# Hash bits of a group's first head copied within SBUF instead of through DRAM, with a shorter warm-up: attention and routed MLP on one Trainium2 core

## The chip, the cores and the metric

The kernel runs on one core of one Trainium2 chip. The metric is the device time of one execution in microseconds (us). Every run quoted here is fast: none was over 1.5% above the fastest of its kernel, the mark beyond which a run is set aside as slow. Times inside an execution come from a profile of one execution and count from the start of its span. The granted clock is the share of TensorE's full clock that the profile shows as given to it: 1.00 is full, 0.50 half.

## The reference, cut to what matters

Attention is restricted by a hash: a query sees only the keys whose 6 hash bits equal its own. A routed MLP with 8 experts follows.

```python
q_bits = (np.einsum('bhsd,dk->bhsk', q, proj) > 0)      # 6 bits per query; k_bits the same
mask = q_bucket[:, :, :, None] == k_bucket[:, :, None, :]
scores = np.where(mask, scale * (q @ k^T), -1e9)
attn = softmax(scores); attn_out = attn @ v             # 4 batches, 8 heads, 768 positions, 64 columns
...                                                     # then _moe_ref: Sinkhorn routing, 8 experts
```

## The kernel before

The eight heads of a batch are two groups of four heads, so there are eight groups. A group is 24 units (4 heads x 6 key tiles). A unit is one pair of score matmuls (`st`), one exponential on ScalarE (`pt`) and six value matmuls (`num`). The mask has no instructions of its own: each key and each query is extended from 64 rows to 71 by its bits, so that the score matmul itself pushes down the pairs that differ.

The preparation of a group, `prepare(n)`, runs while the group before is computed. It transposes k and q on VectorE, casts them on GpSimd, copies ("stacks") each head's 32-row pieces into place by DMA, and computes the bits: TensorE hashes (`pr`), VectorE compares (`bt`). The bits of all four heads lie in `bt` in the wrong partitions. They go to a scratch tensor in DRAM (`put_bits`) and come back head by head (`get_bits`).

```python
def eng(name, h):                 # who issues the small transfers
    return nc.scalar if n == 0 and name == "q" and h < 3 else nc.sync
def put_bits():
    bt = d["bt"]
    dss["kq"] = scr.tile([2, 2, HG, 8, HT], F16, tag="ds", name="ds")           # DRAM
    pin(nc.sync.dma_start(out=dss["kq"].rearrange("n j h r t -> (n j h r) t"), in_=bt))
def get_bits(name, h):
    pin(eng(name, h).dma_start(out=d[name][D:KR, h, :].rearrange("r (j t) -> r j t", j=2),
                               in_=dss["kq"]["kq".index(name), :, h, 0:NB + 1, :].rearrange("j r t -> r j t")))
...
fetch(0, "kqv", nc.sync)
warm = ops.tile([P, 512], F32, tag="o", name="warm")
for x in range(42):               # matmuls on nothing: 0.43 us each at first, 0.22 us from 8.9 us on
    if x == 18:
        for _ in prepare(0): pass
    pin(nc.tensor.matmul(warm, ident, ..., start=True, stop=True))
...
for u in range(len(units) + 1):   # u-th unit; i = u % 24; prepare(n + 1) advances at chosen i
    ...
    pts[u + 1] = scores(*units[u + 1])
    values(u - 1 ...)
```

Bulk loads (k, q and v of the next group at 768 KB each, expert weights at 1 MB) are issued by GpSimd. On the page of the kernel before, the queue of its transfers took 46.5% of the time of the core's 16 DMA engines, those of SyncE and ScalarE 7.6% and 0.5%.

The softmax here doesn't subtract the row's maximum and nothing guards it: scores larger than these inputs give would overflow.

## Time and profile before

| | before |
|---|---|
| time, median of 3 runs | 786.95 us (786.22 to 787.77) |
| span of the profiled execution | 783.6 us (785.36 timed) |
| first exponential of groups 0, 1, 2, 3 | 21.26, 42.22, 65.12, 91.05 us |
| from group 3's first exponential to the end | 692.6 us |

The profiled execution was a little faster than every timed run of this kernel.

From the page of the kernel before: the span, TensorE's busy time, the granted clock in tenths over 40 slices, and the chain of work that ended last.

```profile
span 783.6 us, 16645 instructions
...
PE 757.7 (97%) x6286; PEld 521.1 (66%) x6286; DVE 530.2 (68%) x1198; ACT 509.2 (65%) x1022; POOL 310.8 (40%) x314
...
PEclk9979999999999999999999999999999999999999
...
PE 84%; ACT 7%; DVE 4%; DMA 2%; issue 1%; SPq 1%; POOL 1%; ACTq 0%; POOLq 0%; DVEq 0%
```

TensorE is the bound over the whole span: 97% busy, and 84% of the chain that ended last. The 7 in the third slice (39 to 59 us) is the only dent in the clock.

From the timeline of TensorE: start, length, what, count. In brackets stand the idle time before it and what ended it.

```profile
15.55 5.35 PE L600 MATMUL warm<-va,ident 128*128 128x512 f16 x24
20.74 0.81 PE L507 MATMUL st<-qs,ks 71*128 71x384 f16 x4
...
41.64 0.48 PE L507 MATMUL st<-qs,ks 71*128 71x384 f16 x2 [2.08 <-DMA ks<-ds]
```

The scores start as the warm-up ends. At the first head of group 1 TensorE stood still for 2.08 us, until bits came back from DRAM (`ds`).

From the timeline of the DMA issues on SyncE (SPq), the write to DRAM and the read back, for group 1 and then group 2:

```profile
33.91 0.53 SPq L412 DMA_DIRECT2D ds<-bt  x1
...
39.61 0.27 SPq L415 DMA_DIRECT2D ks<-ds  x1
...
55.26 0.35 SPq L412 DMA_DIRECT2D ds<-bt  x1
...
61.98 0.27 SPq L415 DMA_DIRECT2D ks<-ds  x1
```

A read is issued as soon as its write has landed (39.61 after 39.60 us, 61.98 after 61.97 us). So the write took 5.7 us for group 1 and 6.7 us for group 2, both beside bulk loads (DMA share 1.00 and 1.07). For group 0, with no bulk load in the way (share 0.44), it took 1.66 us. Group 2's bits landed at 64.0 us and its first scores began at 64.53 us.

From the stretch table, the 3.41 us before the clock fell and the half-clock time in thirds: stretch, its length, busy us (count) of PE, PEld, DVE, ACT, POOL, then the granted clock, DMA share and GB/s.

```profile
39.59:43.00 3.41, 1.35 (x17) 0.88 (x18) 0.00 (x0) 1.47 (x3) 0.00 (x0) 1.00 0.16 40
43.00:46.41 3.41, 3.33 (x29) 2.31 (x29) 3.35 (x5) 2.85 (x5) 2.18 (x3) 0.50 0.27 69
46.41:49.83 3.42, 3.42 (x29) 2.16 (x27) 0.56 (x2) 2.30 (x4) 2.81 (x5) 0.50 0.83 277
49.83:53.24 3.41, 3.41 (x25) 1.06 (x24) 0.75 (x2) 1.26 (x2) 2.25 (x4) 0.50 1.02 218
```

After the stretch with the wait the clock is at half for 10.24 us (43.00 to 53.24 us). Group 1 takes 22.9 us from its first exponential to the next group's; group 0, without its wait, took 18.9.

### The profile page before, as it was taken

How to read it: one execution, taken by the hardware profiler on the slowest of the kernel's cores; microseconds unless marked ns; L12 is line 12 of the kernel's file. 1: busy time of each engine (PE TensorE's matmuls, PEld its weight loads, DVE VectorE, ACT ScalarE, POOL GpSimd, SP SyncE). 2: the span in 40 equal slices, each digit the busy share in tenths (PEclk: the TensorE clock that was granted, in tenths of full speed). 3: DMA queues.
4: the chain of work that ended last, by engine and by line, in shares of the span. 5: the costliest groups of instructions: out<-in, count | busy, mean ns of one | idle time of the engine just before them, and what ended most of it. 6: DMA issues, size and time to landing. Idle time of an engine off the chain costs nothing.

```text
span 783.6 us, 16645 instructions
## 1 busy us (share of the span) xinstructions
PE 757.7 (97%) x6286; PEld 521.1 (66%) x6286; DVE 530.2 (68%) x1198; ACT 509.2 (65%) x1022; POOL 310.8 (40%) x314
## 2 busy tenths in 40 slices
PE   6989999999999999999999999999999999999996
PEld 2556656666654676677777777777777777777763
DVE  3435646654449877777777777777777777777774
ACT  0868767677854777766666666666666666666660
POOL 5745346437500133344434334333444443324220
PEclk9979999999999999999999999999999999999999
DMA  5976557463003364486468647764864496443335
GB/s 148 256 167 180 133 164 186 121 151 87 2 1 55 54 108 82 88 155 109 88 111 153 108 82 132 132 115 81 150 119 93 94 166 109 81 82 82 82 82 134
DMA packets 42088, 88.56 MB, mean 113 GB/s; under 512 B 7384, under 2 KB 22360, under 8 KB 42008
## 3 DMA queue, kind: packets, MB, share of 16 engines
q0 software_dynamic: 27440, 71.06, 46.5%
q1 hardware_dynamic: 13545, 15.33, 7.6%
q10 hardware_dynamic: 1023, 1.11, 0.5%
q8 instruction: 49, 0.80, 0.4%
q14 instruction: 31, 0.25, 0.1%
HBM read 53.14 MB, written 7.08 MB: 77 GB/s over the span
## 4 chain that ended last, share of the span: by engine, by line
PE 84%; ACT 7%; DVE 4%; DMA 2%; issue 1%; SPq 1%; POOL 1%; ACTq 0%; POOLq 0%; DVEq 0%
PE a L725 18%; PE a L249 17%; PE d L725 13%; PE y L249 9%; PE st L507 6%; PE d L249 4%; PE hp L565 4%; ACT pt L510 4%; PE num L523 3%; PE yp L575 3%; PE pr L396 2%; PE hp L322 1%; ACT acc L240 1%; PE yp L306 1%; DVE hT L734 1%
## 5 line engine op out<-in xcount | busy, mean ns | idle before, releaser
L734 DVE CUSTOM_DVE_ANT_0 hT<-d,u 128x384 f16<-128x384 f32 x336 | 185.6, 553 | 96.2 <-ACT u L730 95.5
L253 ACT ACTIVATE vt<-a,p 128x256 f32<-128x256 f32 x324 | 153.6, 474 | 148.7 <-PE a L249 148.5
L510 ACT ACTIVATE pt<-st 128x768 f16<-128x768 f32 x192 | 146.4, 809 | 64.7 <-PE st L507 45.4
L730 ACT COPY u<-a 128x384 f32<-128x384 f32 x336 | 161.2, 480 | 23.5 <-PE a L725 19.9
L288 POOL DMA_DIRECT2D acc<-vt x72 | 61.4, 853 | 267.9 <-ACT vt L253 112.8
L249 PEld LDWEIGHTS <-hT 128*128 128x128 f16 x1296 | 126.3, 97 | 50.7 <-DVE hT L734 1.1
L249 PE MATMUL a<-t,hs 128*128 128x256 f16 x972 | 145.8, 272 | 2.0 <-ACT vt L253 1.5
L249 PEld LDWEIGHTS <-hs 128*128 128x128 f16 x972 | 94.8, 98 | 38.3 <-issue 2.8
L725 PEld LDWEIGHTS <-t 128*128 128x128 f16 x896 | 87.7, 98 | 36.3 <-issue 0.6
L725 PE MATMUL d<-xd,t 128*128 128x384 f16 x448 | 109.4, 326 | 0.3 <-DVE hT L734 0.3
L725 PE MATMUL a<-xT,s 128*128 128x384 f16 x448 | 109.4, 326 | 0.1
L507 PE MATMUL st<-qs,ks 71*128 71x384 f16 x384 | 96.0, 332 | 7.1 <-ACT pt L510 3.5
L249 PE MATMUL y<-t,hT 128*128 128x256 f16 x648 | 97.1, 272 | 0.0
L257 DVE SCALAR_TENSOR_TENSOR acc<-y,p,acc 128x256 f32<-128x256 f32 x162 | 77.5, 478 | 11.4 <-PE y L249 11.4
L523 PEld LDWEIGHTS <-pt 128*128 128x128 f16 x1152 | 61.8, 99 | 27.6 <-issue 2.2
L725 PEld LDWEIGHTS <-s 128*128 128x128 f16 x672 | 65.5, 98 | 17.5 <-issue 2.3
L523 PE MATMUL num<-va,pt 128*128 128x65 f16 x1152 | 67.8, 195 | 0.6 <-ACT pt L510 0.6
L764 ACT ACTIVATE hT<-a 128x384 f16<-128x384 f32 x112 | 54.1, 483 | 1.8 <-PE a L725 1.7
L725 PE MATMUL a<-xd,s 128*128 128x384 f16 x224 | 54.3, 323 | 0.8 <-ACT u L730 0.6
L725 PE MATMUL d<-xT,t 128*128 128x384 f16 x224 | 54.7, 326 | 0.0
L725 PE MATMUL a<-xT,t 128*128 128x384 f16 x224 | 54.7, 326 | 0.0
L507 PEld LDWEIGHTS <-ks 71*128 71x128 f16 x384 | 33.8, 99 | 30.5 <-issue 16.4
(100 smaller groups left out, 954.7 us busy)
## 6 DMA issues: line engine op xcount, KB each, us to landing
acc<-vt POOLq DMA_DIRECT2D x72, 512.0 KB, 4.7
t<-in_moe_w_dram POOLq DMA_DIRECT2D x24, 512.0 KB, 7.2
acc<-in_k_dram POOLq DMA_DIRECT2D x7, 768.0 KB, 5.6
acc<-in_q_dram POOLq DMA_DIRECT2D x7, 768.0 KB, 12.1
v<-in_v_dram POOLq DMA_DIRECT2D x28, 192.0 KB, 5.4
out_dram<-acc SPq DMA_DIRECT2D x82, 64.0 KB
t<-in_moe_w_dram POOLq DMA_DIRECT2D x4, 1024.0 KB, 10.9
ks<-t SPq DMA_DIRECT2D x64, 48.0 KB
```

What stands on the lines that cost most here:

```text
L249: pin(nc.tensor.matmul(dst, hq[hn][:, fo, :], wq[wn][:, fo, :], start=first and fo == 0, stop=fo == FH - 1, skip_group_check=True))
L253: pin(nc.scalar.activation(out=vt[:, k], in_=a, func=Act.Copy, scale=p))
L257: pin(nc.vector.scalar_tensor_tensor(out=dst, in0=src, scalar=p, in1=dst, op0=Alu.mult, op1=Alu.add))
L288: pin(nc.gpsimd.dma_start(out=acc[:, b, i], in_=vt, accum_op=Alu.add))
L507: pin(nc.tensor.matmul(st[:, i, 0:HT], d["k"][0:KR, h, kt * P:(kt + 1) * P], d["q"][0:KR, h, i * HT:(i + 1) * HT], start=True, stop=True))
L510: pin(nc.scalar.activation(out=pt, in_=st[:, :, 0:HT], func=Act.Exp, scale=scale))
L523: pin(nc.tensor.matmul(num[:, j * (D + 1):(j + 1) * (D + 1)], pf[:, j * P:(j + 1) * P], va[:, h, kt, :], start=(kt == 0 and j == 0), stop= ...
L565: pin(nc.tensor.matmul(hp[:, 0:HT], w1[:, do, fo * P:(fo + 1) * P], xT[:, do, b * S + t * HT:b * S + (t + 1) * HT], start=(do == 0), stop= ...
L725: pin(nc.tensor.matmul(bk, wq[wn][:, do, f * P:(f + 1) * P], xq[xn][:, do, :], start=first and do == 0, stop=do == 1, skip_group_check=True))
L730: pin(nc.scalar.copy(t, bk))
L734: pin(add(TENSOR_ADD_SAT, out=dst, in0=bk, in1=u, s0=3e38, s1=0.0))
L764: pin(nc.scalar.activation(out=hT[:, f, hi], in_=a, func=Act.Relu))
```

## The change

The intent is to shorten the way of the bits that are needed first. Head 0 of groups 0, 1 and 2 gets its bits by four small copies straight from `bt`. The DRAM way remains for the other heads. The warm-up loses 8 matmuls before the first hash and 2 after it, and ScalarE issues q's heads 0 and 1 of group 0 only; head 2 goes to SyncE.

```diff
-            return nc.scalar if n == 0 and name == "q" and h < 3 else nc.sync
+            return nc.scalar if n == 0 and name == "q" and h < 2 else nc.sync
 ...  # get_bits now always on nc.sync
+        def move_bits(name):
+            for x in range(2):
+                p = 64 * "kq".index(name) + 32 * x
+                pin(eng(name, 0).dma_start(out=d[name][D:KR, 0, x * HT:(x + 1) * HT], in_=d["bt"][p:p + NB + 1, :]))
 ...
+        if n < 3:
+            move_bits("k")
+            move_bits("q")
         put_bits()
         if n == 0:
             stack("k", 1)
             stack("q", 1)
-            for h in range(2):
-                get_bits("k", h)
-                get_bits("q", h)
+            get_bits("k", 1)
+            get_bits("q", 1)
 ...
-        for h in range(2 if n else 0):
+        for h in range(1 if n < 3 else 0, 2 if n else 0):
             get_bits("k", h)
             get_bits("q", h)
 ...
-    for x in range(42):
-        if x == 18:
+    for x in range(32):
+        if x == 10:
```

More of the change, by code (lines that the diff above doesn't have):

```diff
@@ L414, in get_bits @@
         def get_bits(name, h):
-            pin(eng(name, h).dma_start(out=d[name][D:KR, h, :].rearrange("r (j t) -> r j t", j=2),
+            pin(nc.sync.dma_start(out=d[name][D:KR, h, :].rearrange("r (j t) -> r j t", j=2),
                                        in_=dss["kq"]["kq".index(name), :, h, 0:NB + 1, :].rearrange("j r t -> r j t")))
+        def move_bits(name):
+            for x in range(2):
+                p = 64 * "kq".index(name) + 32 * x
+                pin(eng(name, 0).dma_start(out=d[name][D:KR, 0, x * HT:(x + 1) * HT], in_=d["bt"][p:p + NB + 1, :]))
         def cast_v():
```

## The prediction

> **What bounds the kernel now.** TensorE: the page has PE busy 97% of 783.6 us (786.95 timed), and the chain that ended last is PE for 84%. The change touches only the first 70 us, where three stretches are lost to something else:
> 1. Start. The first score matmul is at 20.74 us (timeline). By the stretch table, warm-up fills PE before it: 18 matmuls to 10.68 us (0.43 us each cold, 0.22 warm), the key hash (1.48 us), 24 more from 15.55 to 20.9 us. By semaphore landings the first head's bits arrive at 19.6 to 20.4 us. VectorE waits 3.5 us for the key hash, though q landed at 9.57 us.
> 2. Head 0 of group 1. PE idles 2.08 us (39.56 to 41.64 us; waits view: "PE st <- DMA ks<-ds"). Its bits left VectorE at 33.86 us; the write to DRAM took 33.91 to 39.60 us behind bulk loads, the read back 1.4 us.
> 3. Then the granted clock falls to 0.50 (42.96 to 53.2 us, stretch table). [...] six 65-column matmuls went from 0.35 to 0.54 us[...]. From first exponential to the next group's, group 1 takes 22.9 us; group 0, warm, 18.9 without its stall: 3.9 us lost.
>
> **What the change does.** It removes 10 warm-up matmuls, 8 of them before the key hash, which is then bound by the transposes (8.62 us) or the tenth warm-up (8.75 us): 1.8 us earlier, with q's transposes and hash behind it. For head 0 of groups 0 to 2, two DRAM hops (1.66 + 1.8 us quiet, 5.7 + 1.4 loaded) become one hop of four small copies (estimate 1.5 us quiet, 5 to 6 loaded; 0.3 to 0.6 us of issue each). The DRAM write follows them, needed only for head 1, 4.4 us later. ScalarE issues 6 transfers instead of 9; SyncE takes q's head 2, which delays q's head 3, whose landing (29.72 us) releases the next group's casts.
>
> **On the critical path.** Start: scores at about 18.7 us, set by the warm-up's end (bits at 16.7): -1.9 us; only -0.5 if the clock stays cold. Group 1: consumers come 2 us earlier, data 1 to 1.7, the skipped hop gives 1.5 to 2: stall about 1 us (-1). Clock: so short a stall probably doesn't halve it (60%): -3.9 if so, -2.3 expected. Group 2: the copies land just in time. All of it carries to the end, as later work is paced by PE. Sum about -5 us.
>
> **Predicted: 782.0 us, range 778.0 to 786.8; faster by over 2% 0.02, within 2% 0.97, slower 0.01.**
>
> **What would show it.** First score matmul at 18 to 19.5 us; PE's wait at group 1 under 1.3 us; granted clock 1.00 from 40 to 55 us; group 1 about 19 us; after 70 us only shifted; ds no longer releasing head 0.
>
> **What would make it wrong.** [...] 22 second-burst matmuls at 0.43 us would then end as late as before. The copies queue behind the same stacked transfers and bulk loads ([...] SyncE copies took 1.9 us quiet, 5 to 7 us beside bulk loads), so the stall may stay at 2 us, and the half clock with it: about 785.

Passages that no trace or run of this case shows are cut, where marked. -1.9 (start), -1 (wait at group 1) and -2.3 us (clock) make -5.2, called about -5. In the case that heads "what would make it wrong" the clock stays cold after the first ten warm-up matmuls. In the profile of the kernel before, the clock stayed at 1.00 after a wait of 1.82 us during the warm-up (12.09 to 13.91 us) and fell after the one of 2.08 us at group 1.

## The result, and the profile after

| | before | after |
|---|---|---|
| time, median of 4 runs each | 786.59 us (786.16 to 787.77) | 781.97 us (780.54 to 782.59) |
| ratio, 95% interval | | 0.9936 (0.9918 to 0.9955) |
| span of the profiled execution | 783.6 us | 780.0 us |
| first exponential of group 0 | 21.26 us | 18.54 us (-2.72) |
| group 0: to group 1's first | 20.95 us | 23.39 us (+2.44) |
| group 1: to group 2's first | 22.90 us | 19.40 us (-3.50) |
| group 2: to group 3's first | 25.93 us | 26.03 us (+0.10) |

Ratios here and below are the mean time of one kernel's fast runs over that of the other's of the same rounds, so they are not quite the ratio of the quoted medians. The time fell by 0.6%, which counts as the same at the 2% mark but lies clear of 1. The last four rows add up to -3.7 us, as the two spans differ; the timed medians differ by 4.6 us, as the profiled execution of the kernel before was faster than its timed runs.

The page after:

```profile
span 780.0 us, 16636 instructions
...
PE 754.0 (97%) x6276; PEld 519.0 (67%) x6276; DVE 531.3 (68%) x1198; ACT 509.1 (65%) x1022; POOL 310.6 (40%) x314
...
PEclk9899999999999999999999999999999999999998
...
PE 83%; ACT 8%; DVE 4%; issue 2%; POOL 1%; DMA 1%; SPq 0%; ACTq 0%; POOLq 0%; DVEq 0%
```

The dent in the clock is still there. It has moved from the third slice to the second. TensorE's timeline after:

```profile
13.26 4.92 PE L607 MATMUL warm<-va,ident 128*128 128x512 f16 x22
18.02 0.82 PE L514 MATMUL st<-qs,ks 71*128 71x384 f16 x4
...
28.34 0.80 PE L514 MATMUL st<-qs,ks 71*128 71x384 f16 x2 [1.79 <-DMA qs<-ds]
```

The start came 2.7 us earlier and the wait at group 1 is gone. In its place stands a new wait of 1.79 us, at the first scores of head 2 of group 0, for q's bits. That is the head which the change handed from ScalarE to SyncE. SyncE's issues around it:

```profile
18.36 1.17 SPq L390 DMA_DIRECT2D qs<-t  x2
19.58 1.55 SPq L390 DMA_DIRECT2D ks<-t  x2
21.17 0.53 SPq L415 DMA_DIRECT2D ks<-ds  x1
21.75 0.32 SPq L415 DMA_DIRECT2D qs<-ds  x1
```

Head 2's q bits were issued at 21.75 us and landed at 28.21 us, with group 1's bulk loads under way since 18.52 us. Before, ScalarE issued them at 20.29 us, ahead of the bulk loads (20.82 us), and they landed at 22.16 us.

The stretch table after, the 3.41 us before the clock fell and the two halves of the half-clock time:

```profile
24.80:28.21 3.41, 1.65 (x23) 1.07 (x21) 2.83 (x5) 2.47 (x4) 0.64 (x1) 1.00 1.06 231
28.21:31.62 3.41, 3.28 (x21) 1.31 (x22) 0.56 (x1) 0.81 (x1) 2.64 (x5) 0.50 0.74 150
31.62:35.03 3.41, 3.41 (x26) 1.30 (x24) 1.93 (x4) 1.24 (x2) 3.41 (x6) 0.50 1.32 276
```

The pair of wait and half clock that stood at 40 to 53 us stands at 26 to 35 us now. The last lines are SyncE's for group 2, followed by its first scores, which waited for nothing:

```profile
52.73 1.53 SPq L421 DMA_DIRECT2D ks<-bt  x2
54.36 1.43 SPq L421 DMA_DIRECT2D qs<-bt  x2
55.84 0.44 SPq L412 DMA_DIRECT2D ds<-bt  x1
56.42 1.20 SPq L390 DMA_DIRECT2D ks<-t  x2
62.10 0.28 SPq L415 DMA_DIRECT2D ks<-ds  x1
```
```profile
60.74 0.48 PE L514 MATMUL st<-qs,ks 71*128 71x384 f16 x2
```

The four copies landed at 58.09 to 59.77 us. The DRAM write behind them landed at 62.09 us, so by that write head 0 would have had its bits at about 64 us (an estimate; head 1's landed at 64.3 to 64.5 us), more than 3 us after the scores began. The run moves_g01 below has no copies ahead of the write: 63.55 us.

### The profile page after: what moved, and what is told of

The parts are those of the page before. It is cut to its first block, busy times and chain, and to the rows that moved or that the text cites. A ratio compares the mean times of both kernels' runs of the same rounds, so it can differ in the third digit from the quotient of the medians.

```text
span 780.0 us, 16636 instructions
## 1 busy us (share of the span) xinstructions
PE 754.0 (97%) x6276; PEld 519.0 (67%) x6276; DVE 531.3 (68%) x1198; ACT 509.1 (65%) x1022; POOL 310.6 (40%) x314
## 4 chain that ended last, share of the span: by engine, by line
PE 83%; ACT 8%; DVE 4%; issue 2%; POOL 1%; DMA 1%; SPq 0%; ACTq 0%; POOLq 0%; DVEq 0%
PE a L732 18%; PE a L249 17%; PE d L732 13%; PE y L249 9%; PE st L514 6%; ACT pt L517 5%; PE d L249 4%; PE hp L572 4%; PE num L530 3%; PE yp L582 3%; PE pr L396 2%; PE hp L322 1%; ACT acc L240 1%; PE yp L306 1%; DVE hT L741 1%
## 5 line engine op out<-in xcount | busy, mean ns | idle before, releaser
L517 ACT ACTIVATE pt<-st 128x768 f16<-128x768 f32 x192 | 146.2, 809 | 61.2 <-PE st L514 44.3
L737 ACT COPY u<-a 128x384 f32<-128x384 f32 x336 | 161.2, 480 | 22.9 <-PE a L732 20.3
## 6 DMA issues: line engine op xcount, KB each, us to landing
acc<-in_q_dram POOLq DMA_DIRECT2D x7, 768.0 KB, 11.8
```

The lines of the kernel that those rows point to most:

```text
L517: pin(nc.scalar.activation(out=pt, in_=st[:, :, 0:HT], func=Act.Exp, scale=scale))
L737: pin(nc.scalar.copy(t, bk))
```

## The experiments

The total came out as predicted, but by another way: a late wait gone, an early one come. The question is which part of the change bought the 0.6%. The theories at the outset: (S) the start and the skipped hop at group 1 are two gains that add up; (I) the new wait at head 2 comes from the hand-over to SyncE and costs what it shows; (C) the half clock is a cost of its own. Their rivals say that each group waits for its own data, whatever its predecessor gains.

Twelve kernels were run in three batches, each with 5 rounds beside the kernel before, on three further chips. On these the kernel before was slower and more scattered (medians 788.5 to 788.7 us, 785 to 793 us) than on the first. All results are correct. The granted clock of the kernel before was 0.982 to 0.995 there, mostly lower in the slower runs, against 0.991 in the one profile of the kernel before, from the first chip. So its executions differ in how much half clock they hold, and what that profile shows, the half microsecond of slack at group 2 too, is one execution; none was profiled on these chips. The columns g0 to g3 are the first exponentials of the groups in the profiled execution, in us; the last column is where the clock was at half after it had first come up, in the first 100 us.

| run | ratio (95%) | g0 | g1 | g2 | g3 | half clock, us |
|---|---|---|---|---|---|---|
| before | 1 | 21.26 | 42.22 | 65.12 | 91.05 | 43.0-53.2 |
| after | 0.9936 (0.9918-0.9955) | 18.54 | 41.93 | 61.33 | 87.36 | 28.2-35.0 |
| after_again | 0.9940 (0.9908-0.9973) | 21.40 | 44.97 | 64.37 | 90.66 | 13.7-17.2, 30.8-37.6 |
| warm_only | 0.9989 (0.9956-1.0022) | 18.65 | 40.41 | 62.78 | 92.23 | 38.7-45.5, 62.6-72.8 |
| moves_only | 0.9940 (0.9912-0.9968) | 22.31 | 42.59 | 62.84 | 91.91 | 43.7-47.1, 91.5-94.9 |
| moves_g01 | 0.9995 (0.9966-1.0023) | 18.88 | 41.19 | 64.69 | 92.51 | 28.9-32.3, 63.0-69.9 |
| moves_g12 | 0.9935 (0.9915-0.9955) | 18.46 | 42.66 | 61.70 | 87.65 | 28.1-34.9 |
| moves_g2 | 0.9932 (0.9913-0.9950) | 19.00 | 43.85 | 63.02 | 88.98 | 29.1-36.0 |
| before_hot | 1.0001 (0.9969-1.0032) | 21.68 | 43.08 | 66.83 | 97.14 | 64.3-78.0 |
| keepwarm | 0.9930 (0.9904-0.9956) | 19.71 | 43.00 | 64.52 | 90.44 | 44.3-51.1 |
| gets_first | 0.9980 (0.9951-1.0008) | 18.32 | 43.48 | 67.00 | 92.93 | 27.8-31.2, 41.4-55.1 |
| act3 | 0.9926 (0.9903-0.9950) | 19.41 | 43.22 | 62.27 | 89.11 | 20.8-34.5 |
| act3_hot | 0.9918 (0.9893-0.9943) | 20.43 | 40.17 | 59.86 | 86.70 | none |
| act3_hot_m4 | 0.9926 (0.9903-0.9948) | 20.36 | 41.43 | 63.40 | 89.34 | 39.9-50.1 |

The profiled executions of moves_only, before_hot, keepwarm and act3 were the slowest of their six (787.88, 791.38, 784.71 and 783.58 us), those of moves_g01 and moves_g12 the fastest (786.51 and 781.95 us).

### warm_only: the shorter warm-up alone

```diff
 # on the kernel before
-    for x in range(42):
-        if x == 18:
+    for x in range(32):
+        if x == 10:
```

> The kernel before with the shorter warm-up alone (32 matmuls, the first hash after 10); bits still go by DRAM, ScalarE still issues 9 transfers. Theory S (the start and the group-1 hop are two separate gains): first exponential about 2.5 us earlier (18.5 to 19 us instead of 21.26), because the warm-up's end, not the bits, set the start; the idle of about 2 us at the first head of group 1 and the half clock after it (group 1 about 22.9 us long) stay; total about -2.5 us. Rival M (the start came from the moved bits): first exponential at 20 us or later, total 0 to -1 us. Head 2 of group 0 has no idle, since ScalarE still issues its q.

Measured: 787.33 us median, ratio 0.9989. The start came 2.6 us earlier, as Theory S had it, and head 2 didn't wait. But the gain is not to be told from zero. TensorE's waits for DMA in this profile:

```profile
39.52 0.80 PE L507 MATMUL st<-qs,ks 71*128 71x384 f16 x2 [2.58 <-DMA ks<-ds]
62.20 0.48 PE L507 MATMUL st<-qs,ks 71*128 71x384 f16 x2 [1.51 <-DMA ks<-t]
```

Group 2 still began 2.3 us earlier than before (62.78 against 65.12 us). It waited 1.51 us at its first head, the clock halved there, and group 2 took 29.45 us instead of 25.93. What the start had given was lost in group 2, a place that the prediction had not priced.

### moves_only: the moves alone

```diff
 # on the changed kernel: ScalarE's share (h < 3, and get_bits by eng) and the warm-up (42, 18) as before
-            return nc.scalar if n == 0 and name == "q" and h < 2 else nc.sync
+            return nc.scalar if n == 0 and name == "q" and h < 3 else nc.sync
-            pin(nc.sync.dma_start(out=d[name][D:KR, h, :]...
+            pin(eng(name, h).dma_start(out=d[name][D:KR, h, :]...
-    for x in range(32):
-        if x == 10:
+    for x in range(42):
+        if x == 18:
```

> The changed kernel with the old warm-up (42, hash after 18) and ScalarE issuing q's heads 0 to 2 as before: only the moves within SBUF are new. Theory S: start unchanged (first exponential about 21.2 us), no idle at head 2 of group 0 (its q bits issued by ScalarE, landing by about 22 us), no idle of more than 0.5 us at the first head of group 1, no half clock between 20 and 60 us; group 0 and group 1 about 19 us each; total about -5.5 us. Rival M: first exponential at 19.5 us or earlier.

Measured: 783.96 us median, ratio 0.994, the same as the whole change. The start was not earlier (22.31 us), so Rival M is out. But groups 0 and 1 were not free of waits, as Theory S had it: TensorE waited at the first head of group 1 and the clock halved once between 20 and 60 us.

```profile
41.67 0.48 PE L514 MATMUL st<-qs,ks 71*128 71x384 f16 x2 [1.07 <-DMA qs<-bt]
```
```profile
40.27:43.68 3.41, 1.90 (x26) 1.24 (x25) 0.59 (x2) 2.14 (x4) 0.33 (x1) 1.00 0.25 72
```

Later in the same profile, that of the slowest of the six runs, group 3, whose head 0 still went by DRAM, waited 2.09 us at its first scores (91.22 us), and the clock halved there too: the same loss one group further on.

So the moves carry the gain and the start needn't contribute. Which of the three moves is told by the next runs.

### moves_g01, moves_g12 and moves_g2: which group's move counts

```diff
 # on the changed kernel; the range of get_bits changed to match
-        if n < 3:
+        if n < 2:            # moves_g01;   n in (1, 2) for moves_g12;   n in (2,) for moves_g2
             move_bits("k")
             move_bits("q")
```

> The changed kernel with the moves left out for group 2 alone (its head 0 goes by DRAM again). Theory W (the move for group 2 is what lets the earlier groups' gain reach the end): TensorE waits 1 us or more for group 2's first bits, as in the run with the shorter warm-up alone (1.5 us), the clock may halve after it, and group 2 starts or runs 1.5 to 5 us later than in the changed kernel; total -0.5 to -3 us against before. Rival N (group 2's move does nothing): no wait there, total as the changed kernel within 1 us.

> The changed kernel with the moves left out for group 0 alone (its head 0 goes by DRAM again; shorter warm-up and SyncE's share kept). Theory W (group 0's move is idle, since the warm-up's end sets the start and groups 1 and 2 wait for their own data): first exponential within 0.5 us of the changed kernel's for the same clock phase, no wait over 0.5 us at the first heads of groups 1 and 2, total 0.992 to 0.996 of before. Rival Z (all three moves count): first exponential over 1 us later after the warm-up's end and total within 2 us of before.

> The changed kernel with the moves left out for groups 0 and 1, kept for group 2 alone. Theory X (the move for group 1 counts as well): TensorE waits 1 us or more for DMA at the first head of group 1, and the clock may halve after it, so that group 1's first or last exponential is 1 to 4 us later than with both moves; total -0.5 to -3 us against before. Rival Y (group 2's move alone carries the gain, since group 1 in the changed kernel is slowed by group 0's wait at head 2 anyway): no wait over 0.5 us at the first head of group 1, total as the changed kernel, 0.992 to 0.996.

Measured: without group 2's move, 0.9995: the whole gain is gone (787.80 us median). Without group 0's, 0.9935; with group 2's alone, 0.9932 (783.12 and 783.17 us, same chip). So, beside the shorter warm-up and SyncE's share, which all three runs have, the move for group 2 carries the gain, and the moves for groups 0 and 1 add nothing that these runs can see. In moves_g01 TensorE's waits were

```profile
28.78 0.70 PE L514 MATMUL st<-qs,ks 71*128 71x384 f16 x2 [1.89 <-DMA qs<-ds]
...
63.80 0.80 PE L514 MATMUL st<-qs,ks 71*128 71x384 f16 x2 [3.83 <-DMA ks<-ds]
```

and in moves_g2

```profile
29.46 0.80 PE L515 MATMUL st<-qs,ks 71*128 71x384 f16 x2 [2.45 <-DMA qs<-t]
43.27 0.48 PE L515 MATMUL st<-qs,ks 71*128 71x384 f16 x2 [0.84 <-DMA ks<-ds]
```

The wait of 0.84 us at group 1 lies between what Theory X (1 us or more) and Rival Y (under 0.5 us) had expected; the total sides with Y. The 3.83 us of moves_g01 is the DRAM way of group 2, met by a group 1 that finished on time. This table of landings, read from the profile's semaphore events, shows it (issue to landing, us; for reads and copies the earliest issue and the latest landing of head 0):

```
            write to DRAM     read back         copies in SBUF    first scores of group 2
before      55.26 to 61.97    61.98 to 64.00    -                 64.53, no wait
moves_g01   51.75 to 58.62    58.68 to 63.55    -                 63.80, after 3.83 us of waiting
before_hot  53.77 to 60.83    60.84 to 65.60    -                 65.94, after 4.42 us of waiting
after       (62.09)           -                 52.73 to 59.77    60.74, no wait
```

Both hops ran beside bulk loads. In before, the write landed 0.2 us after the 1 MB of weights (61.97 and 61.74 us) that had been issued 4.5 us ahead of it (50.77 us). The read, 1.4 us for group 1, here lands 0.3 to 0.4 us after the q load behind the weights (63.66 us in before, 63.27 us in moves_g01, 65.21 us in before_hot). Issued earlier, the bits did not arrive earlier by as much: with the write issued 3.5 us earlier than in before they landed 0.45 us earlier in moves_g01, and with 1.5 us earlier they landed 1.6 us later in before_hot. The two hops together took 8.7 to 11.8 us, the four copies of the single hop 7.0 us.

### before_hot: the kernel before, with the half clock of group 1 taken away

```diff
 # on the kernel before, in the main loop, ahead of scores(*units[u + 1])
+            if u + 1 == 24:
+                hot = ops.tile([P, 512], F32, tag="o", name="hot")
+                for x in range(10):
+                    pin(nc.tensor.matmul(hot, ident, vas[0]..., start=True, stop=True))
```

> The kernel before with 10 more warm-up matmuls (about 2.2 us at full clock) in TensorE's order just before the first scores of group 1, where it idles 2.1 us. They take no wait away. Theory C (the half clock after the idle is itself a cost of about 3.9 us): the clock stays 1.00 from 40 to 60 us, group 1 takes about 19 to 20 us instead of 22.9. If that reaches the end, the total is about -3.5 us; if the next group's bits, which came by DRAM with 0.6 us to spare, hold group 2 up instead (rival W), the first head of group 2 waits 1.5 us or more for DMA, the half clock comes there, and the total is within 1.5 us of before.

Measured: 788.48 us median, ratio 1.0001. Theory C is right about the clock: it stayed at 1.00 until 64.3 us, and group 1 ran at the warm pace (19.3 us without the wait at its end, against 22.9 us). Rival W is right about the total: group 2's first head then waited 4.42 us, and the clock halved there.

```profile
65.94 0.80 PE L507 MATMUL st<-qs,ks 71*128 71x384 f16 x2 [4.42 <-DMA qs<-t]
```
```profile
53.77 0.35 SPq L412 DMA_DIRECT2D ds<-bt  x1
...
60.84 0.27 SPq L415 DMA_DIRECT2D ks<-ds  x1
```

This and moves_g01 show the same thing in two ways. In the profile of the kernel before, two limits on group 2's start stood within half a microsecond: TensorE, slowed by the half clock in group 1, and the bits by DRAM. Both runs eased the first limit only: TensorE was ready for group 2 at 61.52 us here and at 59.97 us in moves_g01, against 64.53 us, and the bits stayed on the DRAM way. Neither gained (1.0001 and 0.9995). The changed kernel eases both limits, and so does moves_g2. The reverse, faster bits for group 2 with TensorE as late as before, was not run. That it would gain nothing is argued from the profile, where group 2 did not wait; it is not shown.

### keepwarm and act3: the new wait at head 2

```diff
 # keepwarm, on the changed kernel: 9 matmuls as in before_hot, at u + 1 == 12
 # act3, on the changed kernel: ScalarE's share as before (the first two pairs of lines of moves_only)
```

> The changed kernel with 9 more warm-up matmuls (about 1.9 us at full clock) in TensorE's order just before the first scores of head 2 of group 0, where TensorE now idles 1.8 us for the q bits. Theory C (the idle itself costs about 1.8 us and the half clock that it causes another 2.6 us): group 0's data wait stays (gap between exponentials about 2 us), but the clock stays 1.00 from 20 to 40 us and the rest of group 0 runs at the warm pace; group 0 takes about 20.8 us instead of 23.4; total about -7 us against before. Rival D (the clock is not what made the later part of group 0 slow, or later waits absorb it): total as the changed kernel within 1 us, or group 1's first head waits instead by 2 us or more.

> The changed kernel with one part undone: ScalarE issues q's stacks and bits of heads 0 to 2 again, as before the change. Theory I (the new idle of 1.8 us at head 2 of group 0 and the half clock after it come from handing q's head 2 to SyncE, which then issues its bits 3.2 us after the bulk loads began): the idle at head 2 goes, the clock stays 1.00 between 20 and 60 us, group 0 takes about 19 us instead of 23.4; the first exponential comes up to 0.5 us later, as ScalarE has more to issue; total about -7.5 us against before, -3.5 to -4 against the changed kernel. Rival B (the bulk loads' earlier start alone is the cause, whoever issues): the idle at head 2 stays over 1 us, total as the changed kernel, about -4.6 us.

Measured, keepwarm: 783.39 us median, ratio 0.993, as the changed kernel. The clock stayed at 1.00 to 44.3 us and the rest of group 0 ran warm, but then group 1 waited for its own copies, and the clock halved there:

```profile
42.42 0.48 PE L514 MATMUL st<-qs,ks 71*128 71x384 f16 x2 [2.18 <-DMA qs<-bt]
```

That is Rival D. In the changed kernel the wait at head 2 with its half clock costs little in the total: without it, group 1 had a wait in its place.

Measured, act3: 782.98 us median, ratio 0.9926. The wait at head 2 is gone (TensorE did not idle there), though group 1's bulk loads began as early as in the changed kernel (18.31 us, against 18.52), so it did come from the hand-over, and Rival B is out. But another idle took its place. ScalarE was still issuing transfers when the first scores were ready, and its first exponential came at 19.41 us. TensorE idled 1.72 us, and the clock was at half from 20.8 to 34.5 us:

```profile
17.40:20.81 3.41, 1.69 (x15) 0.89 (x13) 0.00 (x0) 1.40 (x3) 3.33 (x7) 1.00 0.63 151
```

The change to ScalarE's share traded one idle for another. The gap of -3.5 to -4 us against the changed kernel that Theory I had expected is not there.

### gets_first: the bits of group 0 issued ahead of its stacks

```diff
 # on the changed kernel, group 0 only; the later get_bits of heads 2 and 3 left out for n == 0
-            get_bits("k", 1)
-            get_bits("q", 1)
+            for h in range(1, HG):
+                get_bits("k", h)
+                get_bits("q", h)
```

> The changed kernel with one order changed: for group 0, SyncE reads the bits of heads 1, 2 and 3 back from DRAM in a row (six small reads) before the stacks of heads 2 and 3, so all are issued before or as the bulk loads begin. Theory O (the idle at head 2 came from its bits being issued behind the bulk loads): that idle goes or is under 0.5 us, the clock stays 1.00 from 20 to 36 us, group 0 takes 19 to 20.5 us. If group 1's data can be there by then, the total is about -7 us against before; if not (rival G, group 1's start is held by its own data at 41 to 43 us, whatever group 0 does), TensorE waits 1.5 us or more at the first head of group 1 and the total stays within 1 us of the changed kernel.

Measured: 786.76 us median, ratio 0.998: a miss, and worse than the changed kernel. The wait at head 2 became one of 1.35 us for the stack that now came later, and group 1 waited 3.12 us:

```profile
27.68 0.75 PE L517 MATMUL st<-qs,ks 71*128 71x384 f16 x2 [1.35 <-DMA ks<-t]
42.59 0.80 PE L517 MATMUL st<-qs,ks 71*128 71x384 f16 x2 [3.12 <-DMA qs<-bt]
```

Theory O failed: the head needs its stack as well as its bits, and here the stack, now issued later, came last.

### after_again: does the pattern repeat?

> The changed kernel once more, unedited, as the yardstick of this batch and to see whether its pattern repeats. Theory P (the pattern belongs to the kernel): an idle of 1.5 us or more at head 2 of group 0, a half-clock stretch right after it, none at the first heads of groups 1 and 2; group 0 about 23.4 us, group 1 about 19.4, group 2 about 26; total 0.992 to 0.995 of before. Rival V (it was one execution's chance): the idle or the half clock falls elsewhere, with the same total.

Measured: 782.83 us median, ratio 0.994. The pattern belongs to the kernel: a wait of 1.97 us at head 2 (this time the last to land was q's stack, `t`, not its bits), the half clock after it, groups 0 to 2 of 23.57, 19.40 and 26.29 us.

```profile
31.38 0.80 PE L514 MATMUL st<-qs,ks 71*128 71x384 f16 x2 [1.97 <-DMA qs<-t]
```

What did not repeat is the start. The clock came up at 10.3 us and fell to half from 13.7 to 17.2 us, so the first exponential came at 21.40 us, 2.9 us later than in the first profile. This execution ended 3.1 us later than that one. Over the fourteen profiles, in all of which the warm-up begins at about 4.5 us, the clock comes up between 7.2 and 10.3 us.

### act3_hot and act3_hot_m4: a better version?

```diff
 # act3, and 8 matmuls as in before_hot at u + 1 == 2, where TensorE idled while ScalarE issued
 # act3_hot_m4: also "if n < 4" for the moves
```

> ScalarE issues q's heads 0 to 2 as before the change, the moves stay, and 8 warm-up matmuls (1.7 us) stand before the third score pair, where TensorE idled 1.7 us while ScalarE still issued transfers. Theory C2 (in the run without them the clock halved from 20.8 to 34.5 us only because of that idle): the clock stays 1.00 from 17 to 36 us, group 0 takes 19 to 20 us instead of 23.8. Its data rank: group 1's copies should land at about 38.5 us, so a wait of at most 1 us there; total -7 to -9 us against before, the best of all. Rival G (groups 1 to 3 wait for their own data, whatever group 0 does): the wait at the first head of group 1, 2 or 3, or at a later head of group 2, grows by 2 us or more, and the total stays at -4 to -6.5 us.

> As act3_hot, with group 3's head 0 moved within SBUF too. If groups run earlier, group 3's first head (which waited 0.4 us for its read from DRAM in the run with ScalarE's share restored, 2.1 us in the run with the moves alone) is the next to wait: theory W says that wait goes and the total gains up to 2 us on act3_hot; if group 3 has slack or waits for its bulk loads instead, the total is the same within 1 us.

Measured, act3_hot: 781.35 us median (779.54 to 784.83), ratio 0.9918. In the profile Theory C2 is borne out: no half clock at all between 9.3 us and the last microseconds, group 0 in 19.74 us, group 1's first head waiting 0.51 us.

```profile
21.00:36.00 15.00, 14.11 (x172) 8.65 (x171) 7.63 (x12) 13.62 (x20) 10.75 (x17) 1.00 1.08 272
36.00:60.00 24.00, 21.25 (x267) 13.62 (x265) 10.57 (x20) 21.34 (x30) 12.98 (x22) 1.00 0.76 198
```

It has the lowest median and ratio of all, but its interval overlaps those of the changed kernel and of its batch mates (moves_g12: 0.9935), and two of its six runs were at 784.6 and 784.8 us with a granted clock of 0.991. It is not shown to be faster than the changed kernel. The expected -7 to -9 us did not come: the ratio makes -6.5 us. The gain in group 0 did reach group 2 in the profile (59.86 us), and group 2 then took 26.84 us, with a wait of 0.46 us inside it and one of 0.55 us at group 3's first head.

Measured, act3_hot_m4: 782.65 us median, ratio 0.9926, the same within the scatter. In its profile group 1 waited 1.53 us and the clock halved; group 3 no longer waited. Whether group 3's move is worth anything stays open.

## Why the prediction was right or wrong

The predicted time, 782.0 us, was met (781.97 us), and the range and the class held. That it came out within 0.1 us is luck: the sum that led to it was wrong in its terms, and their errors partly cancelled. In the profiles the start gave -2.7 us where -1.9 was expected, group 0 lost 2.4 us where nothing was expected, and group 1 gave -3.5 us where -3.3 (-1 and -2.3) was expected. That makes -3.7 us, not -5; the timed medians differ by -4.6.

1. **"Start: ... -1.9 us"**. The start was earlier as foreseen (first scores at 18.02 us, expected 18 to 19.5). Its worth was not as foreseen: alone it gives a ratio of 0.9989, not told from 1, and the moves without it give 0.994, as much as the whole change. The branch that it names, "if the clock stays cold", occurred in one of the two profiles of the changed kernel (after_again, at half from 13.7 to 17.2 us).
2. **"Group 1: ... stall about 1 us (-1)"**. The wait at group 1 vanished in both profiles. This was not the skipped hop's doing alone: group 0 had been made late by a wait of its own. Without the moves for groups 0 and 1 the total is the same (0.9932).
3. **"Clock: ... -2.3 expected"**. The clock stayed at 1.00 from 40 to 55 us, as the prediction asked. But the half clock had only moved to 28.2 to 35.0 us, after the wait at head 2 of group 0. The prediction had seen that SyncE's larger share would delay "q's head 3"; head 2 itself was hit.
4. **"Group 2: the copies land just in time."** True, and priced at nothing. This is the term without which the gain is gone: 0.9995 without it, 0.9932 with it as the only move (both with the shorter warm-up).
5. **"All of it carries to the end."** This is the step that failed. A gain in groups 0 and 1 carries only as far as the next group whose data isn't there: in warm_only, before_hot and moves_g01 TensorE was ready for group 2 3.0 to 4.6 us earlier than in the kernel before and lost that there, to a wait and the half clock that went with it; keepwarm spared group 0 its half clock and lost it at group 1's first head.

In short, the prediction had most of the facts about each stretch right and added them up, but TensorE's work is not the only chain: each group starts when TensorE and its data are both there.

Open points: whether group 2's move alone, on the kernel before without the shorter warm-up, gives the whole gain; how much the shorter warm-up adds to the moves (the runs only bound it, at about 2 us either way); and whether act3_hot is faster than the changed kernel.

## What to carry to other kernels

Before adding up the gains of several stretches, ask for each consumer how much slack its data has if the consumer comes earlier: in the profile it was half a microsecond at group 2, and easing one of two limits that stand so close only handed the wait to the other. Here a small transfer took 1.9 us when issued ahead of the bulk loads and 6.5 us when issued behind them, so count the hops that meet them and issue it ahead of them. An idle of 2.1 us on TensorE was dearer than its length: the group with the half clock after it took 22.9 us, and 19.3 us where the half clock was kept away (before_hot, without the wait at its end). But taking only the half clock away moved the wait to the next place where data was late (4.42 us at group 2 in before_hot, 2.18 us at group 1 in keepwarm).

## What the runs show of the clock and of small transfers

- Half-clock stretches here are 3.41, 6.83, 10.24 and 13.65 us long. TensorE was not idle throughout before them: in the 3.41 us before the clock fell it was busy for 1.35 (before), 1.65 (after), 1.69 (act3) and 1.90 us (moves_only), with a wait of 1.07 to 2.08 us in each. The clock held after 3.41 us of act3_hot with 2.80 us busy, and after waits of 0.84 us (moves_g2, 43.27 us) and 1.05 us (moves_only, 67.70 us). Neither the busy time nor the wait alone tells the two apart: during the warm-up of the kernel before, the clock held after 1.59 us busy, with a wait of 1.82 us (10.50 to 13.91 us). What tells them apart is not shown.
- TensorE's being busy did not bring the clock back at once. In the kernel before, TensorE was busy for 3.33 and 3.42 us of two stretches (43.00 to 49.83 us) and the clock stayed at half through a third one, to 53.24 us. These were score and value matmuls with 71 rows or 65 columns, and the busy time of matmuls is modelled in the profile; why it took so long is open.
- Small copies took 1.9 us quiet, and mostly 5 to 7 us beside bulk loads. The issue time decided here what was ahead of the loads: q's bits of head 2, issued at 20.29 us by ScalarE, landed at 22.16 us; issued at 21.75 us by SyncE, they landed at 28.21 us. The bulk loads began 2.3 us earlier in the second case; in act3, where they began as early (18.31 us), ScalarE issued these bits at 18.87 us, and TensorE did not wait at head 2.
- The issue time differed with the shape of the transfer. On SyncE a copy of 7 rows from SBUF to SBUF mostly took 0.69 to 0.80 us to issue, a read of 7 rows in two pieces from DRAM mostly 0.27 to 0.53 us, a stack of 32 rows mostly 0.51 to 0.60 us; on ScalarE the 7-row copies took 1.30 and 0.75 us. The four copies of one head hold SyncE for 3.1 us, the four reads of two heads for 1.3 us.
